# The first two x slabs in loads of their own, W1's first slab in halves, and the second x slab's transposes between matmuls

## Chip, cores, metric

One core of one Trainium2 chip. The time is device microseconds of one execution; a kernel is timed in several executions, next to executions of the kernel before on the same chip. Times from single records are rounded to 0.01 us; the recorded texts sometimes have 0.01 less.

## The reference, cut to what matters

`x` is 2048 x 640. One branch is a gated state-space layer, the other a dense layer with GELU; the output mixes them. The head of the program computes the first part of the dense layer, for the first quarter (512 rows) of x:

```
x = A_x                                    # [1, 2048, 640]
g = _sigmoid((x * gate_w).sum(-1, keepdims=True))
a = _A_ref(x, ...)                         # B projection, scan over time, C projection
h = jnp.einsum("bsd,df->bsf", x, w1) + b1  # w1: [640, 1728]   <- the head works here
h = _gelu(h)
b = jnp.einsum("bsf,fd->bsd", h, w2) + b2
return g * a + (1 - g) * b
```

640 is five slabs of 128 (k = 0 to 4). A matmul contracts one slab of x with one slab of W1, and eight output blocks (jf = 0 to 7) accumulate in the eight PSUM banks while k goes outermost.

## The kernel before

x must be transposed, 128 columns to the partitions. For the first quarter, slabs 0 and 1 come by one plain load and are transposed on TensorE; slabs 2, 3 and 4 come by transposing DMA loads. A slab here is 128 of the 640 columns of x, or the 128 rows of W1 that go with them. All loads of x and W1 in the head go out on SyncE's queue, in the order of `prio` (code cut here and below; `...` marks what is left out):

```python
KN = 2
load("xna", "sp", "l_xna", xn[0][:, :, 0:KN * 128], x2[0:512, 0:KN * 128].rearrange(...), ["xna"], 0, ...)   # 256 KB
w1load(0, "sp", 1)                         # W1 slab k=0, columns 0 to 1023, 256 KB
w1load(1, "sp", 1.3)                       # k=1
xtrans(0, range(KN, KN + 1), 1.6, 0.8)     # x slab 2, transposing load, 128 KB
w1load(2, "sp", 2)                         # k=2
xtrans(0, range(KN + 1, KD), 3, 1.3)       # x slabs 3 and 4, transposing load, 256 KB
w1load(3, "sp", 4)                         # k=3
w1load(4, "sp", 5)                         # k=4
# ... the remaining columns of W1, then B
```

TensorE first runs matmuls on constants, so that it is busy while nothing has landed. Then it makes the transposes, which VectorE copies out of PSUM, then the real matmuls:

```python
def f_warm():
    for n in (512,) * 6 + (256,):
        t = nc.tensor.matmul(PS[4][:, 0:n], one..., one..., start=True, stop=True)
...
for i, (k, c0, c1) in enumerate(((0, 0, 2), (0, 2, 4), (1, 0, 2), (1, 2, 4))):
    bank = (7, 6, 5, 7)[i]
    # f_xt: two transposes into `bank`;   f_xc: VectorE copies the bank to xT[0][:, k, ...]
    op(f"xt{i}", "pe", ..., ["xna", "ident"], [("bank", bank)], f_xt, prio=(-990, -989, -988, 2.5)[i])
    op(f"xc{i}", "dve", 0.42, [("bank", bank)], [("xT", 0, k, c0)], f_xc, prio=-2000 + i)
...
# m1_first: (k, jf) = (0,0) (0,1) in halves of 256 columns, (0,2) ... (0,6), (1,0) ... (1,6), (0,7), (1,7), (2,0) ... (4,7)
```

A small list scheduler turns the priorities into one fixed order per engine.

## Time and profile before

The first three executions took 213.09 to 213.74 us, median 213.72. The page of the profiled execution, first lines and the chain that ended last (by engine, then by line; share of the span):

```profile
span 211.5 us, 3140 instructions
...
PE 208.1 (98%) x1266; PEld 121.2 (57%) x1276; DVE 189.3 (90%) x264; ACT 111.3 (53%) x201; POOL 3.0 (1%) x11
...
PE 98%; issue 0%; DVE 0%
PE ps L772 27%; PE ps L642 22%; PE ps L821 21%; PE ps L685 20%; PE ps L622 4%; PE ps L400 1%; PE ps L786 1%; PE ps L663 1%; PE ps L412 0%; DVE osb L855 0%; PE ps L431 0%
```

TensorE is busy for 98% of the span and is 98% of the chain. VectorE is busy for 90%, but it is not on the chain. So time counts only if TensorE gets it or loses it, and the change touches only TensorE's first 10 us.

The head, TensorE alone, in order of time (start, length, instruction group; lengths run to the modelled end of the last one):

```profile
start us, us, engine line op out<-in xcount [idle before <-releaser]
0.78 2.93 PE L400 MATMUL ps<-const-bfloat16-1.0 128*128 128x512 bf16 x7 [0.78 <-PEq L968]
3.67 1.06 PE L412 MATMUL ps<-ident,xn 128*128 128x128 bf16 x8
4.57 2.54 PE L622 MATMUL ps<-xT,W1sb 128*128 128x256 bf16 x13
6.95 0.22 PE L431 MATMUL ps<-ident,rows 128*128 128x128 bf16 x1
7.01 6.42 PE L622 MATMUL ps<-xT,W1sb 128*128 128x512 bf16 x28
```

The warm-up runs to 3.7, the eight transposes (L412) to 4.7, and from 4.57 on the real matmuls (L622) follow without a gap. Read as single records: the x slab has landed at 3.63; the first copy out of PSUM runs from 4.10 to 4.40; a 512-column matmul issues every 0.427 us at first and every 0.216 us after about 4.4. W1's slabs land shortly before they are needed: k=1 at 5.73, and the weight load of the first k=1 matmul is at 5.88; k=3 at 9.45, and its weight load is at 9.60.

The DMA engines in four stretches of the head (window; sum and PE busy us, then PEld, DVE, ACT, POOL, each with its instructions; clock, DMA share, GB/s). The clock column prints 1.00 even before 4.4; the half rate is read from the distance of the matmuls, as above:

```profile
core 0: us, PE busy (x) PEld busy (x) DVE busy (x) ACT busy (x) POOL busy (x), PEclk, DMA share, GB/s
0.00:3.60 3.60, 2.82 (x7) 0.90 (x7) 0.49 (x3) 1.05 (x1) 1.49 (x9) 1.00 0.44 140
3.60:4.40 0.80, 0.80 (x7) 0.55 (x6) 0.30 (x2) 0.23 (x1) 0.00 (x0) 1.00 0.63 118
4.40:5.80 1.40, 1.40 (x11) 0.91 (x11) 0.67 (x3) 0.00 (x0) 0.00 (x0) 1.00 1.09 291
5.80:9.00 3.20, 3.20 (x18) 1.47 (x16) 1.38 (x7) 1.25 (x3) 0.00 (x0) 1.00 1.10 292
```

### The profile page before, as it was taken

To read this page: it belongs to the slowest core of one execution; us is meant where nothing else is said; L and a number is where in the kernel's file an instruction comes from. 1 tells how busy PE (TensorE), PEld (TensorE's weight loads), DVE (VectorE), ACT (ScalarE), POOL (GpSimd) and SP (SyncE) were. 2 spreads that over 40 slices of the span, in tenths; PEclk is the share of its full clock that TensorE was granted. 3 is DMA by queue.
4 is the path that set the end of the run, shared out by engine and by line. 5 is a ranking of instruction groups with operands and counts; after the bars stand their busy time and mean duration, and the time that the engine had idled before them with its cause. 6 is when DMAs were issued, how large, how long until landed. Compare 5 with 4: busy or idle time off the path is not lost.

```text
span 211.5 us, 3140 instructions
## 1 busy us (share of the span) xinstructions
PE 208.1 (98%) x1266; PEld 121.2 (57%) x1276; DVE 189.3 (90%) x264; ACT 111.3 (53%) x201; POOL 3.0 (1%) x11
## 2 busy tenths in 40 slices
PE   8999999999999999999999999999999999999996
PEld 4444444444567776444466777544446777767775
DVE  2599999999999999999999969899999999899444
ACT  2588556678904334556953333456792444723330
POOL 2000000000000010000000001000000000000000
PEclk9999999999999999999999999999999999999999
DMA  5999699999100013100000014100000000010011
GB/s 164 290 246 183 158 225 300 303 213 197 42 0 3 31 38 120 62 0 0 0 3 0 0 48 143 39 23 3 0 0 2 3 31 31 31 34 0 31 34 62
DMA packets 31350, 16.35 MB, mean 77 GB/s; under 512 B 23144, under 2 KB 30440, under 8 KB 31336
## 3 DMA queue, kind: packets, MB, share of 16 engines
q1 hardware_dynamic: 30960, 14.83, 28.5%
q0 software_dynamic: 320, 1.31, 2.0%
q8 instruction: 10, 0.16, 0.3%
q14 instruction: 4, 0.03, 0.1%
q10 hardware_dynamic: 56, 0.01, 0.0%
HBM read 7.63 MB, written 2.62 MB: 48 GB/s over the span
## 4 chain that ended last, share of the span: by engine, by line
PE 98%; issue 0%; DVE 0%
PE ps L772 27%; PE ps L642 22%; PE ps L821 21%; PE ps L685 20%; PE ps L622 4%; PE ps L400 1%; PE ps L786 1%; PE ps L663 1%; PE ps L412 0%; DVE osb L855 0%; PE ps L431 0%
## 5 line engine op out<-in xcount | busy, mean ns | idle before, releaser
L772 PE MATMUL ps<-W2sb,Gl 128*128 128x320 bf16 x416 | 59.2, 299 | 0.0
L772 PEld LDWEIGHTS ps<-W2sb,Gl 128*128 128x128 bf16 x416 | 40.4, 98 | 17.1 <-issue 1.1
L642 PE MATMUL ps<-xT,W1sb 128*128 128x512 bf16 x215 | 47.5, 379 | 0.3
L821 PE MATMUL ps<-CT,H 128*128 128x320 bf16 (+2 forms) x330 | 45.5, 295 | 0.0
L725 DVE TENSOR_TENSOR_SCAN W<-atab,V 128x1280 bf16<-128x1280 f32 x16 | 44.3, 2811 | 0.3
L685 PE MATMUL ps<-xT,BT 128*128 128x512 bf16 x196 | 43.1, 379 | 0.3 <-issue 0.2
L821 PEld LDWEIGHTS ps<-CT,H 128*128 128x128 bf16 x330 | 31.9, 98 | 11.7
L800 ACT ACTIVATE E<-ps,g1col 128x320 bf16<-128x320 f32 x32 | 16.3, 526 | 39.7 <-PE ps L772 25.6
L642 PEld LDWEIGHTS ps<-xT,W1sb 128*128 128x128 bf16 x220 | 21.5, 98 | 26.0
L649 ACT ACTIVATE Gl<-ps,cols 128x512 bf16<-128x512 f32 x44 | 29.6, 688 | 10.0 <-PE ps L642 10.0
L685 PEld LDWEIGHTS ps<-xT,BT 128*128 128x128 bf16 x200 | 19.4, 98 | 23.5 <-ACT Gt L671 0.4
L694 ACT ACTIVATE U<-ps 128x512 bf16<-128x512 f32 x40 | 23.8, 597 | 15.0 <-PE ps L685 14.9
L832 ACT ACTIVATE E<-ps,gcol 128x320 bf16<-128x320 f32 x30 | 15.8, 527 | 22.6 <-PE ps L821 22.6
L759 ACT ACTIVATE ps<-b2b 128x320 f32<-128x320 bf16 x32 | 14.1, 441 | 1.1
L481 DVE TENSOR_TENSOR osb<-xg,E 128x640 bf16<-128x640 bf16 x15 | 7.3, 487 | 7.9 <-ACT E L832 7.6
L842 DVE SCALAR_TENSOR_TENSOR xg<-xn,gcol,dsk 128x640 bf16<-128x640 bf16 x16 | 13.9, 882 | 0.4
L597 DVE SCALAR_TENSOR_TENSOR scr<-xn,gwb 128x640 bf16<-128x640 bf16 x16 | 13.2, 822 | 0.4
L481 DVE TENSOR_TENSOR H<-H,V 128x1280 bf16<-128x1280 bf16 x16 | 12.5, 821 | 0.3
L481 DVE TENSOR_TENSOR V<-V,W 128x1280 bf16<-128x1280 bf16 x16 | 12.5, 821 | 0.3
L481 DVE TENSOR_TENSOR V<-mr,U 128x2560 bf16<-128x2560 bf16 x8 | 11.9, 1488 | 0.2
L481 DVE TENSOR_TENSOR H<-c,W 128x2560 bf16<-128x2560 bf16 x8 | 11.9, 1488 | 0.2
L481 DVE TENSOR_TENSOR W<-mi,U 128x2560 bf16<-128x2560 bf16 x8 | 11.9, 1483 | 0.0
(80 smaller groups left out, 99.9 us busy)
## 6 DMA issues: line engine op xcount, KB each, us to landing
out_dram<-osb SPq DMA_DIRECT2D x15, 160.0 KB, 1.8
W2sb<-in_B_w_dram SPq DMA_DIRECT2D x1, 2080.0 KB, 8.9
W1sb<-in_B_w_dram SPq DMA_DIRECT2D x5, 256.0 KB, 3.9
xn<-in_A_x_dram POOLq DMA_DIRECT2D x2, 640.0 KB, 4.6
xn<-in_A_x_dram SPq DMA_DIRECT2D x1, 640.0 KB, 7.9
W1sb<-in_B_w_dram SPq DMA_DIRECT2D x1, 480.0 KB, 5.8
W1sb<-in_B_w_dram SPq DMA_DIRECT2D x1, 400.0 KB, 6.5
xn<-in_A_x_dram SPq DMA_DIRECT2D x1, 384.0 KB, 6.0
```

What stands on the lines that cost most here:

```text
L481: return inc("dve", nc.vector.tensor_tensor(out=o, in0=a, in1=b, op=o_))
L642: t = nc.tensor.matmul(PS[bank][:, :], W1sb[:, k, jf * 128:(jf + 1) * 128], xT[q][:, k, :], start=(k == 0), stop=(k == KD - 1))
L649: return inc("act", nc.scalar.activation(Gl[q % 2][:, jf, :], PS[bank][:, :], ACT.Gelu_apprx_tanh, bias=b1col[:, jf:jf + 1]))
L685: t = nc.tensor.matmul(PS[bank][:, :], BT[:, ci, kd, k * 128:(k + 1) * 128], xT[q][:, kd, :], start=(kd == 0), stop=(kd == KD - 1))
L694: return inc("act", nc.scalar.activation(dst, src, ACT.Copy, scale=1.0 if ci == 0 else -1.0))
L725: t = inc("dve", nc.vector.tensor_tensor_scan(out=g[:, ci, :], data0=a, data1=v[:, ci, :], initial=0.0, op0=ALU.mult, op1=ALU.add))
L759: return inc("act", nc.scalar.activation(PS[bank][:, 0:HALF], b2b[:, cols], ACT.Copy))
L772: t = nc.tensor.matmul(PS[bank][:, 0:HALF], Gl[q % 2][:, jf, t4 * 128:(t4 + 1) * 128], W2sb[:, jf, cols], start=False, stop=False, skip_gr ...
L800: return inc("act", nc.scalar.activation(E1[c % NE][:, cols], PS[bank][:, 0:HALF], ACT.Copy, scale=g1col[:, c:c + 1]))
L821: t = nc.tensor.matmul(PS[bank][:, 0:n], H[b % NHB][:, ci, k, s * 128:(s + 1) * 128], CT[:, ci, k, cols], start=(i == 0), stop=(i == 2 * K ...
L832: return inc("act", nc.scalar.activation(E2[c % NE][:, cols], PS[bank][:, 0:HALF], ACT.Copy, scale=gcol[:, c:c + 1]))
L842: return inc("dve", nc.vector.scalar_tensor_tensor(out=xg[c % 2][:, :], in0=xn[q % 2][:, c % 4, :], scalar=gcol[:, c:c + 1], in1=dsk[:, :] ...
```

## The change

The intent: half of the x slab should land sooner than the whole of it, so TensorE needs one warm-up matmul less and starts real work earlier. The second x slab comes in a load of its own and is transposed between matmuls. W1's first slab is cut in halves, so that its first half is there in time.

```diff
-        load("xna", "sp", "l_xna", xn[0][:, :, 0:KN * 128], x2[0:512, 0:KN * 128].rearrange(...), ["xna"], 0, dur=0.45, lat=2.0)
-        w1load(0, "sp", 1)
+        for k in range(KN):
+            load(f"xna{k}", "sp", f"l_xna{k}", xn[0][:, :, k * 128:(k + 1) * 128], x2[0:512, k * 128:(k + 1) * 128].rearrange(...),
+                 [("xna", k)], (0, 1.2)[k], dur=0.45, lat=(2.0, 2.6)[k])
+        for h in range(2):
+            f0, f1 = h * FW // 2, (h + 1) * FW // 2
+            load(f"w1_0{h}", "sp", f"l_w10{h}", W1sb[:, 0, f0:f1], B_w1[0:128, f0:f1], [("w1", 0, h)], prio=1 + 0.1 * h, lat=2.6)
         w1load(1, "sp", 1.3)
 ...
-            for n in (512,) * 6 + (256,):
+            for n in (512,) * 5 + (256,):
 ...
-            op(f"xt{i}", ..., ["xna", "ident"], ..., prio=(-990, -989, -988, 2.5)[i])
+            op(f"xt{i}", ..., [("xna", k), "ident"], ..., prio=(-990, -989, 6.4, 6.5)[i])
+        def f_fill():
+            return inc("pe", nc.tensor.matmul(PS[4][:, 0:192], one..., one..., start=True, stop=True))
+        op("fill", "pe", 0.2, (), [("bank", 4)], f_fill, prio=-980)
 ... (the matmuls' dependences follow the new names)
```

SyncE's order becomes: x slab 0, W1 k=0 first half, second half, x slab 1, W1 k=1, then as before. There are two issues more ahead of W1 k=1. TensorE's order becomes: warm-up, four transposes, a filler, seven matmuls of k=0, four transposes, two matmuls of k=0, k=1 and on.

More of the change, by code (lines that the diff above doesn't have):

```diff
@@ L353, in bass_gated_mix__ssm_conv_s5__dense_activation_gelu__prompt_kernel @@
         KN = 2
-        load("xna", "sp", "l_xna", xn[0][:, :, 0:KN * 128], x2[0:512, 0:KN * 128].rearrange("(c p) d -> p c d", p=128), ["xna"], 0, dur=0.45, lat=2.0)
-        w1load(0, "sp", 1)
+        for k in range(KN):
+            load(f"xna{k}", "sp", f"l_xna{k}", xn[0][:, :, k * 128:(k + 1) * 128], x2[0:512, k * 128:(k + 1) * 128].rearrange("(c p) d -> p c d", p=128),
+                 [("xna", k)], (0, 1.2)[k], dur=0.45, lat=(2.0, 2.6)[k])
+        for h in range(2):
+            f0, f1 = h * FW // 2, (h + 1) * FW // 2
+            load(f"w1_0{h}", "sp", f"l_w10{h}", W1sb[:, 0, f0:f1], B_w1[0:128, f0:f1], [("w1", 0, h)], prio=1 + 0.1 * h, lat=2.6)
         w1load(1, "sp", 1.3)
@@ L413, in f_xt @@
                 return inc("pe", t)
-            op(f"xt{i}", "pe", 0.11 * (c1 - c0), ["xna", "ident"], [("bank", bank)], f_xt, prio=(-990, -989, -988, 2.5)[i])
+            op(f"xt{i}", "pe", 0.11 * (c1 - c0), [("xna", k), "ident"], [("bank", bank)], f_xt, prio=(-990, -989, 6.4, 6.5)[i])
             def f_xc(k=k, pt=pt, c0=c0, c1=c1):
@@ L420, in bass_gated_mix__ssm_conv_s5__dense_activation_gelu__prompt_kernel @@
             op(f"xc{i}", "dve", 0.42, [("bank", bank)], [("xT", 0, k, c0)], f_xc, prio=-2000 + i)
+        def f_fill():
+            return inc("pe", nc.tensor.matmul(PS[4][:, 0:192], one.broadcast_to([128, 128]), one.broadcast_to([128, 192]), start=True, stop=True))
+        op("fill", "pe", 0.2, (), [("bank", 4)], f_fill, prio=-980)
         XK0 = [[("xT", 0, k)] for k in range(KD)]
@@ L569, in bass_gated_mix__ssm_conv_s5__dense_activation_gelu__prompt_kernel @@
         load("xnb", "sp", "l_xnb", xn[0][:, :, KN * 128:D], x2[0:512, KN * 128:D].rearrange("(c p) d -> p c d", p=128),
-             [("xn", 0, 0), ("xn", 0, 1)], 32.4, dur=1.0, lat=6.0, reads=["xna"])
+             [("xn", 0, 0), ("xn", 0, 1)], 32.4, dur=1.0, lat=6.0, reads=[("xna", k) for k in range(KN)])
         load("w2a", "sp", "l_w2a", W2sb[:, 0:NF - 1, :], B_w2[0:nmain, :].rearrange("(j p) d -> p j d", p=128), ["w2a"], prio=33, lat=8.0)
@@ L623, in f_mm @@
                                                       start=(k == 0 and t0 == 0), stop=(k == KD - 1), skip_group_check=jf < 2))
-                op(f"m1_0_{jf}_{k}_{t0}", "pe", d_mm(t1 - t0), (XK0[k] if h is None else XK0[k][h:h + 1]) + [("w1", k)], [("bank", jf)],
+                op(f"m1_0_{jf}_{k}_{t0}", "pe", d_mm(t1 - t0), (XK0[k] if h is None else XK0[k][h:h + 1]) + ([("w1", k)] if k else [("w1", 0, jf // (NW // 2))]), [("bank", jf)],
                    f_mm, prio=pe_prio())
@@ L644, in f_mm @@
                     return inc("pe", t)
-                op(f"m1_{q}_{jf}", "pe", KD * d_mm(512), XT[q] + ([("w1", k) for k in range(KD)] if jf < NW else [("w1", "r", int(jf * 128 >= FM))]), [("bank", bank)], f_mm, prio=pe_prio())
+                op(f"m1_{q}_{jf}", "pe", KD * d_mm(512), XT[q] + ([("w1", k) for k in range(1, KD)] + [("w1", 0, 0), ("w1", 0, 1)] if jf < NW else [("w1", "r", int(jf * 128 >= FM))]), [("bank", bank)], f_mm, prio=pe_prio())
                 def f_ge(jf=jf, bank=bank):
```

## The prediction

> **What bounds it now.** The page gives a span of 211.5 us with TensorE busy 98%; the chain that ended last is TensorE for 98% of the span, almost without gaps after the first 5 us. The change touches only the head.
>
> **The head before (timeline, single records, landings).** Warm-up matmuls run from 0.78 us and issue every 0.427 us (512 columns); the last ends its issue slot at 3.50. The 256 KB x slab is issued at 0.74 and has landed at 3.62. Transposes start at 3.67, one each 107 ns; the copies out of PSUM take 0.29 us each, the first 4.10 to 4.39. The first real matmul issues at 4.57, and from there TensorE is dense. The granted clock goes to full at 4.39: before it 512 columns take 0.427 us, after it 0.216: the cold and warm rate of the Trainium skill, "TensorE: Matmul & The Clock Gate", Part 1. The weight slabs come just in time: the second (k=1) lands at 5.73 and is needed at about 5.8; the fourth lands at 9.45 and is needed at about 9.7.
>
> **What the change does.**
> 1. Half of the x slab goes first. 512 descriptors remain, of 256 instead of 512 bytes. Transposing packets of 256 bytes took 18 ns, 512-byte packets 27: 32 descriptors an engine make about 0.3 us less. I estimate landing at 3.2 to 3.35 instead of 3.62.
> 2. One warm-up matmul less: 0.427 us earlier, warm-up over at 3.08.
> 3. First real matmul then at 4.02 to 4.18, that is 0.4 to 0.55 us earlier. But what runs before 4.39 is at half rate, so 0.1 to 0.2 of it is lost again.
> 4. The second slab's four transposes, which hid in the wait for the first copy (0.12 us visible), now stand between matmuls: 4 x 55 ns = 0.22 us. The two matmuls behind them and the first of k=1 wait for their copies: transpose start to copy start 0.32 us, two copies end about 0.75 to 0.8 us after the first transpose, while only two 0.216 us matmuls can fill. I expect a hole of 0.2 to 0.25 us there.
> 5. Two more DMA issues on SyncE's queue, about 0.45 us each, ahead of W1's second slab: issued at about 2.7 instead of 1.79. Bytes ahead of it are the same, and descriptors cost some 0.3 us more per engine, so landing at 6.0 to 6.5 instead of 5.73, needed at about 6.1. Later slabs slip 0.2 to 0.5 us, and the fourth had almost no slack.
>
> Sum: gain 0.3 to 0.4 net of the cold clock, against 0.22 + 0.22 + 0 to 0.4 of new transposes, hole and late weights. Net about 0.1 us slower by the time of k=1, perhaps 0.3 by k=3.
>
> **Prediction:** 213.9 us, 8 in 10 between 213.2 and 214.7 (the three runs before spread over 0.65). Faster by over 2%: 0.005; within 2%: 0.985; slower by over 2%: 0.01.
>
> **What would show it.** First x slab landing near 3.3; first real matmul near 4.1; idle TensorE time of some 0.2 us after the second transposes, released by a VectorE copy; a wait for W1's second or fourth slab that was not there; first matmul of k=1 at 6.1 to 6.5 (before 6.09).
>
> **What would make it wrong.** Full clock granted later because TensorE idles more in the warm-up: a full clock window late would cost over 1 us. Or the stretch from 3.6 to 4.4, where the DMA engines moved only 118 GB/s (windows), fills up in the new order, so slabs come earlier and 0.2 to 0.4 us is gained.

## The result

| | before | changed |
|---|---|---|
| median of six executions | 213.16 us | 213.65 us |
| lowest to highest | 212.76 to 213.74 | 213.50 to 214.29 |
| span of the profiled execution | 211.45 us | 212.37 us |
| ratio | | 1.0024 (95%: 1.0001 to 1.0046) |
| the same, measured again (e1) | | 1.0008 (95%: 0.999 to 1.0027) |

A ratio is the mean time of one kernel's fast runs over that of the other's of the same rounds, so it is not quite the ratio of the medians. With the executions of before from all four series put together (38 fast ones; one at 369.98 us is left out as a disturbance) the mean is 213.23, and the mean of the 12 of the changed kernel is 213.67: 0.44 us or 0.2% slower. But two of these four series ran on other chips, without the changed kernel beside them (their means are 213.00 and 213.32). In the two series that timed both side by side the change costs 0.50 and 0.23 us, 0.34 us with their executions put together (12 against 17; the 95% interval of the second series' ratio alone includes no difference). The fastest of the 12 (213.37) is beaten by 24 of the 38. So the change makes the kernel slower by some 0.2 to 0.5 us, far inside the 2% that count as the same.

The page after:

```profile
span 212.4 us, 3154 instructions
...
PE 209.1 (98%) x1276; PEld 121.1 (57%) x1276; DVE 189.3 (89%) x264; ACT 111.3 (52%) x201; POOL 3.0 (1%) x11
...
PE 94%; SPq 3%; DMA 2%; issue 0%; DVE 0%
PE ps L781 27%; PE ps L651 22%; PE ps L830 20%; PE ps L694 20%; DMA W1sb<-in_B_w_dram 2%; PE ps L631 2%; SPq L326 1%; PE ps L795 1%; SPq L333 1%; PE ps L672 1%; DVE osb L864 0%
```

The chain is no longer TensorE from end to end: 2% of it is a DMA into W1sb, and 3% is SyncE's queue (SPq), issuing. The chain of the head in order of time shows which (start, length, what):

```profile
3.34 1.20 SPq L333
...
4.59 0.58 SPq L326
...
5.21 1.26 SPq L333
...
6.52 4.06 DMA W1sb<-in_B_w_dram
10.58 0.14 issue
10.71 3.61 PE ps L631 x16
```

Followed back from the end, TensorE's long stretch starts at 10.71. It was released by W1's slab k=3, issued at 6.52 and landed at 10.58. Ahead of that issue, SyncE's queue issued with gaps of only 0.04 to 0.06 us. (The issues from 0.74 to 3.3 stand above the lines shown.)

TensorE in the head after, to be held against the timeline of before:

```profile
0.78 2.50 PE L404 MATMUL ps<-const-bfloat16-1.0 128*128 128x512 bf16 x6 [0.78 <-PEq L977]
3.11 0.61 PE L416 MATMUL ps<-ident,xn 128*128 128x128 bf16 x4
3.51 0.37 PE L427 MATMUL ps<-const-bfloat16-1.0 128*128 128x192 bf16 x1
4.07 1.59 PE L631 MATMUL ps<-xT,W1sb 128*128 128x256 bf16 x7 [0.19 <-DVE xT L422]
5.50 0.39 PE L416 MATMUL ps<-ident,xn 128*128 128x128 bf16 x4
5.72 1.76 PE L631 MATMUL ps<-xT,W1sb 128*128 128x512 bf16 x6
7.32 0.22 PE L440 MATMUL ps<-ident,rows 128*128 128x128 bf16 x1
7.38 3.13 PE L631 MATMUL ps<-xT,W1sb 128*128 128x512 bf16 x13
10.71 3.61 PE L631 MATMUL ps<-xT,W1sb 128*128 128x512 bf16 x16 [0.21 <-DMA W1sb<-in_B_w_dram]
```

The first real matmul comes at 4.07 instead of 4.57. But there are now gaps and extra work behind it, and the matmuls up to 4.85 run at half rate. The list, from the records of single matmuls (a hole is a start-to-start distance beyond the regular one; the differences are of unrounded starts):

| from before to changed | us | how it is worked out |
|---|---|---|
| first real matmul | -0.50 | 4.07 - 4.57 |
| half-rate matmuls | +0.34 | four of 256 columns take 0.78 instead of 0.44 |
| four transposes between matmuls | +0.22 | 5.50 to 5.72 |
| hole behind the transposes (VectorE's copy) | +0.22 | 6.16 instead of 5.94 |
| wait for W1 k=1 (landed 6.32) | +0.09 | 6.46 instead of 6.37 |
| wait for W1 k=2 (landed 8.48) | +0.16 | 8.62 instead of 8.45 |
| wait for W1 k=3 (landed 10.58) | +0.37 | 10.71 instead of 10.34 |
| sum | +0.90 | spans: 212.37 - 211.45 = 0.92 |

The whole loss is in these lines, because nothing after the head changes. From the first weight load of the B projection (18.45 before, 19.35 changed) to the end of the span it is 193.00 us before and 193.02 after, and 193.00 to 193.05 in every one of the 14 profiles. That weight load is used below as the **mark**: it tells an execution's span from its head alone. The two lines, before and after:

```profile
18.45 2.47 PEld L685 LDWEIGHTS ps<-xT,BT 128*128 128x128 bf16 x12
```

```profile
19.35 1.61 PEld L694 LDWEIGHTS ps<-xT,BT 128*128 128x128 bf16 x8
```

The DMA engines in the same four stretches:

```profile
core 0: us, PE busy (x) PEld busy (x) DVE busy (x) ACT busy (x) POOL busy (x), PEclk, DMA share, GB/s
0.00:3.60 3.60, 2.82 (x11) 1.18 (x11) 0.55 (x4) 0.97 (x1) 1.50 (x9) 1.00 0.43 95
3.60:4.40 0.80, 0.61 (x5) 0.29 (x3) 0.45 (x2) 0.31 (x1) 0.00 (x0) 1.00 1.10 286
4.40:5.80 1.40, 1.40 (x12) 0.86 (x9) 0.00 (x0) 0.00 (x0) 0.00 (x0) 1.00 1.01 218
5.80:9.00 3.20, 3.14 (x16) 1.18 (x14) 1.54 (x8) 0.88 (x3) 0.00 (x0) 1.00 1.12 204
```

The dip from 3.6 to 4.4 is filled (286 GB/s instead of 118). From 5.8 to 9.0 the engines are as busy as before (1.12 against 1.10 by this count) but move 204 GB/s instead of 292. In the first 3.6 us, too, they are as busy as before (0.43 against 0.44) and move less, 95 GB/s instead of 140. Summed over the first three windows that is 876 KB by 5.8 us instead of 1006 KB (worked out from the lines): the loads, the first ones now in smaller pieces, are 130 KB behind before k=2 is due.

### The profile page after: what moved, and what is told of

The parts are those of the page before. It is cut to its first block, busy times and chain, and to the rows that moved or that the text cites. A ratio compares the mean times of both kernels' runs of the same rounds, so it can differ in the third digit from the quotient of the medians.

```text
span 212.4 us, 3154 instructions
## 1 busy us (share of the span) xinstructions
PE 209.1 (98%) x1276; PEld 121.1 (57%) x1276; DVE 189.3 (89%) x264; ACT 111.3 (52%) x201; POOL 3.0 (1%) x11
## 4 chain that ended last, share of the span: by engine, by line
PE 94%; SPq 3%; DMA 2%; issue 0%; DVE 0%
PE ps L781 27%; PE ps L651 22%; PE ps L830 20%; PE ps L694 20%; DMA W1sb<-in_B_w_dram 2%; PE ps L631 2%; SPq L326 1%; PE ps L795 1%; SPq L333 1%; PE ps L672 1%; DVE osb L864 0%
## 5 line engine op out<-in xcount | busy, mean ns | idle before, releaser
L651 PE MATMUL ps<-xT,W1sb 128*128 128x512 bf16 x220 | 48.1, 379 | 0.0
L694 PE MATMUL ps<-xT,BT 128*128 128x512 bf16 x200 | 43.8, 379 | 0.0
L490 DVE TENSOR_TENSOR V<-s,W 128x2560 bf16<-128x2560 bf16 x8 | 11.9, 1483 | 0.0
```

What stands on the lines that cost most here:

```text
L490: return inc("dve", nc.vector.tensor_tensor(out=o, in0=a, in1=b, op=o_))
L651: t = nc.tensor.matmul(PS[bank][:, :], W1sb[:, k, jf * 128:(jf + 1) * 128], xT[q][:, k, :], start=(k == 0), stop=(k == KD - 1))
L694: t = nc.tensor.matmul(PS[bank][:, :], BT[:, ci, kd, k * 128:(k + 1) * 128], xT[q][:, kd, :], start=(kd == 0), stop=(kd == KD - 1))
```

## The experiments

Theory A: the two extra issues on SyncE's queue make W1's slabs late, and TensorE ends up waiting for them. Rival C: the slabs are late because the DMA engines are the limit, and descriptors of 256 bytes and 1 KB cost them more than those of 512 bytes and 2 KB. Rival B: the full clock is granted later. Rival D: the transposes and the hole behind them set the time, the slabs don't.

Unless it is said otherwise, every other engine keeps its order of instructions. One table for all; "full rate" is the start of the first matmul at the full rate, "first" the first real matmul; k=1, k=2, k=3 are the landings of W1's slabs (the last of 16 engines); one profile each, in us:

| run | full rate | first | k=1 | k=2 | k=3 | mark | median time |
|---|---|---|---|---|---|---|---|
| before | 4.45 | 4.57 | 5.73 | 7.24 | 9.45 | 18.45 | 213.16 |
| e12 before again | 4.10 | 4.64 | 5.74 | 7.34 | 9.78 | 18.54 | 212.86 (one run) |
| changed | 4.85 | 4.07 | 6.32 | 8.48 | 10.58 | 19.35 | 213.65 |
| e1 changed again | 3.55 | 3.95 | 6.34 | 8.64 | 10.44 | 19.21 | 213.54 |
| e2 before + two tiny issues | 4.84 | 4.84 | 5.71 | 7.67 | 10.11 | 18.88 | 213.70 |
| e3 before, 256-byte descriptors | 6.13 | 4.86 | 5.57 | 7.75 | 9.72 | 19.36 | 213.40 |
| e4 changed, x slab 1 on ScalarE | 4.38 | 4.38 | 5.35 | 7.85 | 10.01 | 19.35 | 213.82 |
| e5 changed, W1 k=0 whole | 4.40 | 4.40 | 6.32 | 8.08 | 10.22 | 18.99 | 213.97 |
| e6 changed, transposes earlier | 6.51 | 3.92 | 6.34 | 8.50 | 10.29 | 19.30 | 213.87 |
| e7 before, later W1 slabs on ScalarE | 5.02 | 4.69 | 6.18 | 11.62 | 12.54 | 23.78 | 215.11 (slow profile) |
| e8 e5 + e6 + later W1 slabs on ScalarE | 3.55 | 4.25 | 5.98 | 8.71 | 11.64 | 23.13 | 217.04 |
| e9 before, no x slabs 3, 4 | 4.99 | 4.83 | 5.89 | 8.25 | 10.11 | 18.88 | 213.07 |
| e10 changed, no x slabs 3, 4 | 5.78 | 4.11 | 6.32 | 8.75 | 9.38 | 19.24 | 213.94 |
| e11 e10 + transposes earlier | 4.88 | 4.12 | 6.06 | 8.61 | 9.25 | 19.11 | 213.48 |

Medians of before beside them: 213.48 (e1 to e4), 212.94 (e5 to e8), 213.24 (e9 to e12, without the disturbed one). In e4 and e5 nothing ran when the rate rose: the trace's record of the granted clock has it at 4.17 and 3.89.

The table holds the main finding. In "before again", changed, e1, e2, e5 and e9 the mark is the landing of k=3 plus 8.77 us, and in e10 and e11 the landing of k=2 plus 10.50 us, each to within 0.01. From that slab on TensorE runs at one pace, so its landing sets the span. What TensorE does before it, earlier start, transposes and hole included, only makes the wait for the slab longer or shorter. In the first profile of before no slab holds TensorE (the sum for k=3 would be 18.22, the mark is 18.45). In e3 and e6 the late full rate, in e4 the late x slab holds it longer than k=3 does (sums 18.49, 19.06 and 18.77).

### e1: the changed kernel again

No edit.

> The changed kernel, unaltered, as a second profile. Theory A (the extra issues on SyncE's queue make W1's slabs land later, and the fourth slab sets the time): the fourth slab lands at about 10.6 us again and TensorE waits for it; time 0.3 to 0.9 us over the kernel before. Rival B (the full clock is granted later because TensorE idles more during the warm-up): the full clock comes at about 4.8 us again, never as early as 4.4. If the grant time moves between runs of the same code, B is not a property of the change.

Measured: ratio 1.0008 (0.999 to 1.0027). TensorE in this profile:

```profile
3.55 0.25 PE L427 MATMUL ps<-const-bfloat16-1.0 128*128 128x192 bf16 x1
3.95 1.26 PE L631 MATMUL ps<-xT,W1sb 128*128 128x256 bf16 x7 [0.15 <-DVE xT L422]
...
6.47 1.02 PE L631 MATMUL ps<-xT,W1sb 128*128 128x512 bf16 x4 [0.26 <-DMA W1sb<-in_B_w_dram]
```

The filler (L427) already takes 0.25 us instead of 0.37: the full rate is there at 3.55, 1.3 us earlier than in the first profile of the same code. Yet the mark is only 0.14 us earlier. The line at 6.47 shows why: it waited for a DMA into W1sb. TensorE was ready sooner and waited longer for the slabs: the holes ahead of k=1, k=2 and k=3 are 0.43, 0.31 and 0.08 us. So B falls as a property of the change (the grant moves between executions of one code), and the slabs set a floor, the earliest time that the mark can have, as A and C have it. D fails in these two profiles of the changed kernel: the transposes and the hole (0.44 us) come before the wait for k=3, and no load of the head waits for TensorE, so without them TensorE would only have waited longer.

### e2: before, with two tiny issues

```diff
         w1load(0, "sp", 1)
+        for i in range(2):
+            load(f"tiny{i}", "sp", f"l_tiny{i}", tiny[:, i, :], gate_w[0:512].rearrange("(p d) -> p d", d=32), [("tiny", i)], 1.1 + 0.1 * i, dur=0.0)
         w1load(1, "sp", 1.3)
```

> The kernel before with two tiny loads (1 KB each) issued on SyncE's queue between W1's first and second slab: two more issues, nothing else. Theory A (serial issue): every later slab is issued about 0.9 us later, the second lands at about 6.5 instead of 5.73, the fourth at about 10.4 instead of 9.45; TensorE gets holes and the time grows by 0.7 to 0.9 us. Rival C (the DMA engines are the limit, and the smaller descriptors cost the time): the slabs land within 0.2 us of before, time +0.0 to +0.1 us.

Measured: W1 k=1 was issued 0.98 us later (2.77 instead of 1.79) and landed at 5.71, no later at all. k=2 landed 0.43 us later and k=3 0.66. TensorE waited 0.17 us for k=3, and not for the others. Ratio 1.0016 (0.9997 to 1.0036). Theory A is refuted for k=1: there the issue has slack. It holds in part for k=2 and k=3. The expected 0.7 to 0.9 us did not come; by the mark it is 0.43 us, of which 0.26 is a first matmul that came later (the x slab landed at 3.84 in this execution).

### e3: before, with 256-byte descriptors

```diff
-        load("xna", ..., xn[0][:, :, 0:KN * 128], x2[0:512, 0:KN * 128]..., ["xna"], 0, ...)
+        load("xna", ..., xs[:, :, 0:128], x2[0:1024, 0:128].rearrange("(c p) d -> p c d", p=128), ...)   # xs: idle part of Gl[1]
```

The same 256 KB and one issue; it reads other rows, so the result is wrong (relative error 0.025).

> The kernel before with its one first x load made of 1024 descriptors of 256 bytes instead of 512 of 512 bytes, the same bytes and the same number of issues (wrong result on purpose: it reads other rows). Theory A: W1's slabs land within 0.3 us of before, time +0.0 to +0.3 us. Rival C: W1's fourth slab lands 0.5 us or more later than 9.45 and the time grows by 0.4 to 0.9 us.

Measured: k=1 landed 0.17 us earlier, k=2 0.51 later, k=3 0.27 later; ratio 0.9997 (0.9977 to 1.0017), so no cost in time. Rival C alone falls, too. Its lateness and that of e2 add up to 0.94 us for k=2 and 0.93 for k=3, against 1.24 and 1.13 in the changed kernel: each part seems to make a share, neither the whole. (These are single profiles; k=3 differs by 0.32 between the two of before.)

This profile shows something else. The full rate came at 6.13, 1.28 us after the first real matmul. Half of 1.28 is 0.64; with the first matmul later by 0.28, the mark should be later by 0.92. Measured: 19.36 - 18.45 = 0.91. So the grant (the moment at which the full rate is given) alone can cost 0.64 us, more than the change costs on average.

### e4: x slab 1 issued on ScalarE's queue

```diff
-            load(f"xna{k}", "sp", ...)
+            load(f"xna{k}", ("sp", "act")[k], ...)      # behind ScalarE's four row loads
```

(Shortened: the run moves the finished issue from SyncE's list to ScalarE's.)

> The changed kernel with the second x slab issued on ScalarE's queue instead of SyncE's; same bytes, same descriptors, one issue less on SyncE. Theory A: second, third and fourth W1 slab are issued 0.52 us earlier, the fourth lands at about 10.05 instead of 10.58, first matmul of k=3 at about 10.2; 0.4 to 0.5 us faster than the changed kernel. Rival C: the fourth slab lands at 10.4 or later and the time does not change by more than 0.1 us.

Measured: the W1 slabs were issued 0.53 to 0.55 us earlier and landed 0.98, 0.63 and 0.57 us earlier than in the changed kernel, k=3 at 10.01 as theory A said, and TensorE's waits for W1 k=1 to k=3 were gone. But W1's first half landed at 4.25 instead of 3.93 and held the first real matmul until 4.38, and x slab 1, issued at 2.59, landed only at 6.04 (3.45 us after its issue; 2.60 us on SyncE's queue). TensorE stood still for 0.63 us ahead of its transposes, and the copies' hole followed. Time: ratio to before 1.0021 (1.0002 to 1.004), so the expected 0.4 to 0.5 us was not gained. One wait was exchanged for another.

### e5: W1's first slab whole

```diff
-        for h in range(2):
-            ... load(f"w1_0{h}", ...)
+        load("w1_0", "sp", "l_w10", W1sb[:, 0, 0:FW], B_w1[0:128, 0:FW], [("w1", 0, 0), ("w1", 0, 1)], prio=1, ...)
```

> The changed kernel with W1's first slab loaded whole again: one issue less on SyncE, no 1 KB descriptors; both x slabs stay on SyncE. Theory A+C (issues and small descriptors each add lateness to W1's slabs, and TensorE ends up waiting for them): second, third and fourth slab land about 0.4 to 0.6 us earlier than in the changed kernel (6.3, 8.5, 10.5), the holes ahead of k=2 and k=3 shrink below 0.1 us, 0.2 to 0.4 us faster than it and equal to before within 0.2 us. Rival D (the second slab's transposes and the wait for their copies set the time): no change against the changed kernel.

Measured: k=2 and k=3 landed about 0.4 us earlier than in the changed kernel, but k=1, though issued 0.53 us earlier, at 6.32 again. The first real matmul had to wait for the whole slab (landed 4.27) and came at 4.40, so two thirds of the gained start were gone. In this profile the hole ahead of k=2 is gone, the one ahead of k=3 is 0.18, and the mark (18.99) is 0.36 us earlier than the changed kernel's, as expected, and 0.54 later than before's. The executions do not show this gain. Time: ratio 1.0055 (1.0028 to 1.0082), with two executions at 215.1 that no profile explains. The expectation of "equal to before" was wrong. Why k=1 doesn't come earlier here stays open; its packets and those of the transposing load behind it were moved in the same stretch, 4.6 to 6.2 us.

### e6: the second slab's transposes earlier

```diff
-            prio=(-990, -989, 6.4, 6.5)[i]
+            prio=(-990, -989, 4.4, 4.5)[i]      # right after the four half matmuls
```

(The scheduler's guess for the latency of x slab 1 is also lowered, from 2.6 to 2.0; so too in e8 and e11.)

> The changed kernel with the second slab's transposes moved ahead of three matmuls, so that their copies are done before they are needed. Theory A+C: the hole of 0.22 us behind the transposes goes (or turns into a wait for the second x slab), but W1's fourth slab still lands at about 10.5 and the first matmul of k=3 does not start before 10.5; time unchanged within 0.1 us. Rival D: 0.2 us faster than the changed kernel, all the way to the end.

Measured:

```profile
3.92 1.03 PE L631 MATMUL ps<-xT,W1sb 128*128 128x256 bf16 x4
4.89 0.61 PE L416 MATMUL ps<-ident,xn 128*128 128x128 bf16 x4
5.29 2.68 PE L631 MATMUL ps<-xT,W1sb 128*128 128x512 bf16 x9
```

The nine matmuls behind the transposes (L416) now run in one piece: the hole is gone. The time did not gain: 213.65 to 214.06, ratio to before 1.0039 (1.0025 to 1.0052). In the profiled execution the full rate came only at 6.51, so TensorE was late anyway and waited for no slab; and still the mark (19.30) is where it was with the grant at 4.85 (19.35) and at 3.55 (19.21). Three grants 3 us apart, marks within 0.14: an early grant is eaten by the wait for the slabs, and only a very late one shows. Rival D, 0.2 us faster to the end, did not come true by the times; this one profile can't say why, because its late grant hides what the hole was worth.

### e7 and e8: later W1 slabs issued on ScalarE's queue

e7 is the kernel before, e8 the changed one with W1 k=0 whole and the transposes earlier; in both, W1 k=2, 3 and 4 go out on ScalarE's queue, after W1 k=0 has landed.

```diff
+        HOLD, VIA_ACT = ("w1_0",), ("w1_2", "w1_3", "w1_4")
         def load(name, eng, sem, dst, src, ...):
             def fn():
-                return dma_inc(eng, engines[eng].dma_start(dst, src), sem)
+                if name in VIA_ACT: E.wait("act", <the load named in HOLD>)
+                return dma_inc(eng, engines["act" if name in VIA_ACT else eng].dma_start(dst, src), sem)
```

> The kernel before with W1's third, fourth and fifth slab issued on ScalarE's queue, after the first slab has landed; same bytes. If SyncE's issue order is what makes the slabs late, the fourth lands at 8.7 or earlier instead of 9.45; if the DMA engines are the limit it lands at 9.2 or later. TensorE in before hardly waits for slabs, so the time stays within 0.2 us either way.

> The changed kernel with all three repairs: W1's first slab whole, the second slab's transposes earlier, and W1's third to fifth slab issued on ScalarE's queue after the first slab has landed. Theory A+C: no hole above 0.1 us after the first real matmul (about 4.1 to 4.3), so 0.5 to 0.8 us faster than the changed kernel and 0.1 to 0.4 us faster than before. If holes stay, the DMA engines and not the issues are the limit, and it equals before.

Measured: both were clearly slower, ratios 1.011 (1.0069 to 1.0151) and 1.0171 (1.0149 to 1.0193). The profile of e7 is of an execution in the slow state (218.1 us; the fast ones took 214.53 to 217.44), so it is read for the order of events alone, and e8's, of the fast state, is put beside it. The lines of its chain, then of TensorE's timeline:

```profile
4.32 7.29 DMA W1sb<-in_B_w_dram
11.62 0.14 issue
```

```profile
11.75 4.42 PE L623 MATMUL ps<-xT,W1sb 128*128 128x512 bf16 x12 [3.27 <-DMA W1sb<-in_B_w_dram]
```

W1 k=2 left ScalarE's queue at 4.32 and took 7.29 us to land (3.73 us in before), and TensorE stood still for 3.27 us (the bracket in its line). In e8 k=2 took 4.58 us, k=3 7.11. The transposing load of x slabs 3 and 4 on SyncE's queue took 8.07 us from issue to landing in e7 and 8.65 in e8, against 4.11 in before. After that stop the matmuls issue at half rate again, every 0.43 us; the trace's record of the granted clock has half rate from 11.74 to 15.15 in e7 and from 13.73 to 17.15 in e8. So the low mean clock of the slow execution (0.992) comes from its own stop; e8's profile and e7's execution at 217.44 have 0.992 too. Both expectations were wrong: issuing from a second queue did not relieve the first.

### e9, e10, e11: less for the DMA engines ahead of k=3

```diff
-        xtrans(0, range(KN + 1, KD), 3, 1.3)
+        op("zx", "pool", 1.0, (), [("xT", 0, k) for k in range(KN + 1, KD)], lambda: inc("pool", nc.gpsimd.memset(xT[0][:, KN + 1:KD, :], 0.0)), ...)
```

e9 is this edit on before, e10 on the changed kernel, e11 is e10 with e6's edit. The first quarter's dense layer then lacks two of five slabs; the comparison's tolerance let it pass.

> The kernel before with the transposing load of x slabs 3 and 4 of the first quarter taken away (zeros written once by GpSimd instead; wrong result on purpose), so that the DMA engines have 256 KB of slow 256-byte packets less ahead of W1's fourth and fifth slab. TensorE's instructions and their order are those of before. Theory: before hardly waited for slabs, so it gains at most 0.2 us; the fourth slab lands at 8.5 or earlier instead of 9.45.

> The changed kernel with the same load taken away. Theory (late slabs are what the changed kernel loses by): the waits ahead of k=3 and k=4 go, it is 0.3 to 0.6 us faster than the changed kernel, and what is left of its difference to the kernel before without that load is TensorE's own part: about 0.5 us of earlier start, less the half-rate matmuls, the four transposes, the 0.22 us hole and whatever wait for the second slab is left, so between 0.2 us slower and 0.2 us faster. Rival D (transposes and hole, not slabs): it stays as slow as the changed kernel.

> As the last, with the second slab's transposes moved ahead of three matmuls. With the slabs out of the way the 0.22 us hole is now on the critical path, so taking it away should show: 0.1 to 0.2 us faster than the last kernel in TensorE's matmul times, where it showed nothing as long as the fourth slab was late. If the second slab's landing (about 6.3) then holds k=1, the gain is nearly nil.

Measured: e9 0.9987 of before (0.9967 to 1.0008), e10 1.002 (1.0 to 1.0039), e11 1.001 (0.9988 to 1.0032). In e10, k=3 landed at 9.38 instead of 10.58 and the wait for it was gone, as expected. But the time did not fall below the changed kernel's, and the expectation (0.3 to 0.6 us faster, within 0.2 us of e9) was wrong: the mean of its six executions is 213.78, and 213.09 for e9 on the same chip, 0.69 us apart. So the wait for k=3 was not the only thing that held it. In its profile the full rate came late (5.78), and k=2 landed at 8.75, about when TensorE came to it. A DMA reports its landing engine by engine, and this shows what held k=2: in the changed kernel all 16 engines had done their share between 8.37 and 8.48; in e10 eleven had by 7.57, but the last at 8.75, in e11 twelve by 7.32 and the last at 8.61. So the load taken away had slowed k=2 as well, and a few late engines kept the gain from TensorE. Why they are late is not shown. In e11, where the grant came at 4.88 and the hole was gone, that shows:

```profile
7.11 1.24 PE L631 MATMUL ps<-xT,W1sb 128*128 128x512 bf16 x5
8.75 4.48 PE L631 MATMUL ps<-xT,W1sb 128*128 128x512 bf16 x19 [0.40 <-DMA W1sb<-in_B_w_dram]
```

The first k=2 matmul starts at 8.75, 0.56 us later than its turn, because its slab landed at 8.61. With the hole taken away, the wait for k=2 took its place. e9's k=3 slab landed later than in before (10.11 against 9.45), against my expectation. Here, too, most of it came early: eight engines by 7.87, fifteen by 8.88 (before: fifteen by 8.89). The one at 10.11 set the mark, and why it was late stays open.

### e12: before again

> The kernel before, unaltered, as a second profile: the slabs land within 0.3 us of the first profile (5.73, 7.24, 9.45). If the time the full clock is granted is free of the code, it comes anywhere between 3.5 and 6.6 us, and each microsecond that it comes after the first real matmul (4.57) costs half a microsecond of the span.

Measured, in a single execution (state unknown): 212.86 us; the slabs landed within 0.32 us of the first profile; full rate at 4.10. Its mark is 0.09 later, its first real matmul 0.06. Fifteen engines had k=3 by 9.61 and fourteen by 8.97, the last at 9.78; TensorE waited 0.03 us for it.

### What is settled and what is open

The full rate came between 3.55 and 6.51 us in the 14 profiles, with no relation to the change that could be seen. Settled is that the landing of W1's slabs sets a floor for the mark (8.77 us after k=3, 10.50 after k=2), that the change raises this floor, and that an earlier start can't go below it. In the changed kernel's order of loads (changed, e1, e6) k=2 and k=3 land at 8.5 to 8.6 and 10.3 to 10.6 instead of 7.2 to 7.3 and 9.5 to 9.8, and the marks lie at 19.2 to 19.4, for grants from 3.55 to 6.51. Before has the floor as well, but lower: its second profile sits on it (18.54), its first is just above (18.45 against 18.22). Not settled: how that lateness splits between the two issues, the 256-byte and 1 KB descriptors and the place of x slab 1 in the queue (e2 and e3 give about 0.4 us and 0.5 us of the 1.2 us for k=2, 0.7 and 0.3 of 1.1 for k=3, from one profile each). One or two late engines of the 16 move k=3 by up to 1.2 us (before: fifteen by 8.89, the last at 9.45), so these splits are rough. That the slower half of before's executions had late grants is argued from e3, not shown. No version tried here beats before.

## Why the prediction was right or wrong

The measured median, 213.65 us, lies in the range, and the sign (slightly slower) was right. Part of this is luck. The point, 213.9, was made when only three executions of before were known, with a median of 213.72; six have 213.16. Against the first it forecasts some 0.2 us of slowdown, and the medians show 0.49: a base that was 0.56 us too high made up for that. Before's own median lies just 0.04 below the range. The mechanism is a better test than the number. Point by point:

- **First x slab landing at 3.2 to 3.35:** 3.06, and 3.05 to 3.14 in the later profiles that load it so. Better than I estimated.
- **First real matmul at 4.02 to 4.18:** 4.07. Right.
- **Half-rate loss of 0.1 to 0.2:** 0.34 in this profile, 0 in e1. The step that failed was to take the clock's 4.39 as fixed. It moves by 1.3 us between two profiles of the same code, and by 3 us over all profiles.
- **Four transposes, 0.22 us:** 0.22. **The hole behind them, 0.2 to 0.25:** 0.22, released by VectorE's copy as said. Right as durations. But they are not worth their length in time: in both profiles of the changed kernel TensorE waits for k=3 after them anyway, and that slab's landing sets the mark.
- **W1 k=1 at 6.0 to 6.5, first k=1 matmul at 6.1 to 6.5:** 6.32 and 6.46. The numbers are right, the way to them is not shown: I added the cost of two issues and of smaller descriptors, but each alone moved k=1 by -0.02 (e2) and -0.17 us (e3), and in e5, issued 0.53 us earlier, it landed at 6.32 again. That is luck until it is explained.
- **"Later slabs slip 0.2 to 0.5 us":** this term was mis-sized. k=2 slipped by 1.24 us and k=3 by 1.13 (e1: 1.40 and 0.99). I took the same bytes to mean nearly the same arrival; but the engines, as busy as before, had moved 130 KB less by 5.8 us. The waits it made are 0.62 us of the 0.90 us in the profile, against my "0 to 0.4".
- **Net 0.3 by k=3:** 0.90 in the profiled pair, 0.34 as the mean of the executions timed side by side. Before's fast profile flatters it: a late clock can cost such a kernel 0.64 us (e3; that before's slower executions are of this kind is not shown), while the changed kernel spends an early clock on waiting.
- **What would make it wrong:** the dip from 3.6 to 4.4 did fill up, but the slabs came later, not earlier.

## What to carry to other kernels

When loads arrive just in time, an earlier start on the compute engine buys nothing unless the last loads of the stage come earlier too: look at each later slab's landing and its slack before you cut the first one in pieces. Splitting the first loads can put its price on the loads behind them: here they landed 0.6 to 1.4 us later, with the same bytes ahead of them. When single executions differ by more than the effect, find a mark in the trace that tells the span from the stage in question, and account for the clock first. If the mark follows a landing by a constant (8.77 us here), that landing sets the time.

## What the Trainium skill lacked or had wrong

- **"TensorE: Matmul & The Clock Gate", Part 1** says that the full rate comes around 4 us into sustained matmul work, give or take 0.5 us from run to run, and that the window behind it is free-running (3.4 us). The rates agree (0.427 and 0.216 us for 512 columns). The spread does not: the first full-rate matmul came 2.77 to 5.73 us after the first matmul (at 0.78) in 14 profiles, a spread of 2.96 us. A box of the same part does say that one kernel ran 6, 11 or 14 cold matmuls in different runs, which fits better than its "0.5 us"; and 2.77 us is less than the one busy window that its table asks for. A late grant cost half of the delay: 0.64 us for 1.28 in e3.
- **"DMA: Bandwidth & Descriptors", Issuing engines are not separate DMA queues,** says that issuing from several engines saves only issue time. It lacks that it can cost: a transposing load on SyncE's queue took 8.07 (e7) and 8.65 us (e8) instead of 4.11 while plain loads went out on ScalarE's queue, and the first of these took 7.3 us (e7, a slow execution) and 4.6 us (e8) instead of 3.7.
- **"DMA: Bandwidth & Descriptors", Specifications,** asks for 512 bytes or more for the line rate. In the single packet records a packet of 256 bytes took 18 ns (median), one of 512 bytes 27, one of 1 KB 46 and one of 2 KB 84: 14, 19, 22 and 24 bytes per ns for one engine. The loss of rate is there, but it goes on above 512 bytes, as the fixed cost per packet leads one to expect that the same page names under "Why small descriptors are slow (HBM only)" and works out for 256 bytes alone. At 256 KB in all it did not show in the time (e3: ratio 0.9997).
- **No page** that I found has the delay between a load's issue and its landing for a queue of loads: here W1's slabs of 256 KB took 3.0 to 4.6 us in the two kernels, and in e2 a slab issued 0.98 us later landed no later.
